# Ten instead of six channel blocks of two MLP jobs get their bias on VectorE, under a new written-out order

## The chip, the cores and the metric

One core of a Trainium2 chip. The metric is the device time of one execution in microseconds (us), the median of several runs. The engines are named as in the profile: PE (TensorE matmul) with PEld (its weight loads), DVE (VectorE), ACT (ScalarE), POOL (GpSimd) and SP (SyncE, which issues nearly all DMAs).

## The reference

Two layer kinds run in turn, twice: sliding-window attention (32 heads of 16 channels, a window of 256) and an MLP of 512 to 1792 channels with GELU, each on normalized rows, each added to the residual. There are 2048 rows of 512 channels in bfloat16, and both rounds use the same weights.

```python
def _A_ref(x, wqkv, wo):          # H = 32, Dh = 16, W = 256
    q, k, v = ...                 # x @ wqkv, split by heads
    scores = einsum("bhqd,bhkd->bhqk", q, k) * (Dh ** -0.5)
    mask = (idx[:, None] - idx[None, :] >= 0) & (idx[:, None] - idx[None, :] < W)
    p = softmax(where(mask, scores, -1e9))
    return einsum("bhqk,bhkd->bhqd", p, v) ... @ wo

def _B_ref(x, w1, b1, w2, b2):
    return gelu(x @ w1 + b1) @ w2 + b2

x = x + _A_ref(_layernorm(x), A_wqkv, A_wo)
x = x + _B_ref(_layernorm(x), B_w1, B_b1, B_w2, B_b2)
x = x + _A_ref(_layernorm(x), A_wqkv, A_wo)
x = x + _B_ref(_layernorm(x), B_w1, B_b1, B_w2, B_b2)
```

## The kernel before

**Tiles.** The rows stay on the chip in `X` as 16 tiles of 128 rows; two rounds make 32 tile steps (`tau` 0 to 31). Attention goes by 16 blocks `b` of two tiles. The MLP goes by ten jobs (`JOBS`): jobs 0 and 1 have two tiles each (256 columns), jobs 2 to 7 four (512 columns), jobs 8 and 9 two again.

**Attention of a block.** PE makes scores into pairs of PSUM banks (`sa`, `sb`); ACT takes exp from there into the ring `E` (L948), 304 times over the whole kernel. DVE or POOL multiplies the window's triangular parts by a mask (L969). PE multiplies by V (`od`), DVE transposes the result from PSUM (`TT`, L1034), takes reciprocals (`Rc`), DVE or POOL scales (`TM`, L1039), DVE transposes back (`OT`, L1044), and PE does the out-projection (`op`) that DVE adds to `X` (L790).

**LayerNorm rows** (`layernorm`, L734 to L760). DVE takes the statistics, POOL the power -1/2 (L741), DVE scales into `xn` (L744). For the first tiles PE then transposes the rows with the identity (L36). From `tau` 14 on in the attention layer, and for `tau` 4 to 29 in the MLP layer, VectorE transposes 32x32 blocks into one of four slots `xs_` (L753); SP writes the slot to a scratch tensor in DRAM, `scr_x` (L758), and reads it back in the wanted arrangement into `xnTA` (attention) or `xnTB` (MLP) (L760). Each is one DMA of 128 KB. SP issues in order and waits at the head of its queue: a read behind another waits with it.

**An MLP job** (`mlp`). For each of 14 channel blocks of 128, PE multiplies W1 by the job's rows. The first `NPRE` blocks go through VectorE: it adds the bias while it moves the block from PSUM to `gT` (L1103), and ACT takes GELU of two such blocks at a time from SBUF (L1106). The remaining blocks go to ACT straight from PSUM, bias and GELU in one (L1114). `NPRE` is 6 for all jobs but the last two, which have none. ACT loads a table at each turn from exp to GELU and back. Then PE multiplies by W2 (`y`) and DVE adds to `X`.

**The order** is written out by hand, as three lists that a planner made outside the kernel. `ORDER` names every piece of work once, and each engine executes its pieces in that order. `TURNS` says for each piece that two engines can do (masks, `TM`, some PSUM moves, the copy `xv`, the epsilon) which one does it: 0 is the first choice, DVE throughout, 1 the other. `BANKS` gives each PSUM group its banks. The durations that the code gives to each piece (`dur`) estimate when it starts and ends; in the finished program they only affect which PE instruction carries a wait that comes early, and the order of waits.

Of the kernel before, what the change touches and what calls it, by code (L numbers as in the profile page):

```python
# [298 lines left out]
def bass_interleave_layers__sliding_block__dense_activation_gelu__prompt_kernel(  # L299
# [43 lines left out]
    NXV = 1  # L343
# [16 lines left out]
    def NPRE(J):  # L360
        return 6
# [13 lines left out]
    with ExitStack() as kctx:  # L375
        S_ = _Sched(nc, kctx)

        def sb(name, shape, dtype=dt.bfloat16):
# [18 lines left out]
        xv = sb("xv", [P, NXV, DC, P])  # L397
        b1raw = xv[0:FC, 0, 0, :]
        scr = nc.dram_tensor("scr_x", (NSC, P, D), dt.bfloat16, kind="Internal").ap()
# [233 lines left out]
        add = PL.add  # L633
# [5 lines left out]
            reads=["ident"], writes=["ident"])  # L639
# [518 lines left out]
        B = PL.gmap  # L1158
# [52 lines left out]
```

## Time and profile before

| What | us |
|---|---|
| Median of three runs | 450.91 (450.76 to 451.44) |
| The profiled execution | 454.36 |
| Its span, first to last instruction | 452.6 |
| PE busy | 436.2 |
| ACT busy | 391.5 |
| DVE busy | 365.2 |
| POOL busy | 244.9 |

The rows of the trace come from the profiled execution, which is 3.45 us longer than the median. Busy time of PE is counted from a matmul's start to its modelled end, and neighbours overlap; so a matmul of 512 columns is listed with 380 ns while the next starts 216 ns after it. In a row of the groups the two numbers behind the bar are busy time in us and the mean length of one instruction in ns; behind the next bar stands the idle time of the engine just before them and what ended it. In the windows each engine's busy time stands with its count of instructions; `PEclk` is the granted share of TensorE's full clock.

### The profile page before, as it was taken

The numbers are of one execution on the slowest core, as the hardware profiler recorded it, in microseconds if no ns is written. First come the engines' busy times: TensorE is split into PE (matmuls) and PEld (weight loads), VectorE is DVE, ScalarE is ACT, GpSimd is POOL, SyncE is SP. The second block draws the span as 40 slices with busy tenths as digits, with TensorE's granted clock in tenths as the row PEclk, the third lists the DMA queues.
The fourth block names the chain that finished last, engine by engine and source line by source line (L and its number), as shares of the span: only waits on it lengthen the run. The fifth ranks groups of instructions, "written<-read, shape, count | busy, mean of one in ns | idle before, by whom it ended". The sixth has DMA issues, their size and how long they took to land.

```text
span 452.6 us, 19312 instructions
## 1 busy us (share of the span) xinstructions
PE 436.2 (96%) x8764; PEld 230.9 (51%) x8764; DVE 365.2 (81%) x733; ACT 391.5 (87%) x470; POOL 244.9 (54%) x297
## 2 busy tenths in 40 slices
PE   8999999888989999999999999999999999999997
PEld 5555645545534544554445535445454553445665
DVE  6999979789978889879987989998787787673711
ACT  3999999999969999799998999979998999793352
POOL 5674763626755555553587446662767365665120
PEclk9999999999989999999999999999999999999999
DMA  8920000000130112110040011400121002002102
GB/s 262 369 82 4 4 3 3 4 3 26 38 84 1 38 50 72 38 49 3 25 108 15 13 48 40 96 15 23 50 73 50 3 25 73 26 4 83 48 1 71
DMA packets 39903, 22.88 MB, mean 51 GB/s; under 512 B 24460, under 2 KB 39308, under 8 KB 39820
## 3 DMA queue, kind: packets, MB, share of 16 engines
q1 hardware_dynamic: 39404, 21.24, 16.2%
q8 instruction: 69, 1.13, 1.1%
q10 hardware_dynamic: 416, 0.39, 0.2%
q14 instruction: 14, 0.11, 0.1%
HBM read 13.77 MB, written 7.86 MB: 48 GB/s over the span
## 4 chain that ended last, share of the span: by engine, by line
PE 74%; ACT 13%; DMA 5%; DVE 4%; SPq 1%; issue 1%; POOL 0%; DVEq 0%
PE ps L32 74%; ACT E L948 11%; DMA xnTB<-scr_x 2%; DMA X<-in_A_x_dram 2%; DMA scr_x<-xs_ 1%; DVE stat L734 1%; DVE E L969 1%; SPq L760 1%; ACT gT L1114 1%; DVE xs_ L753 1%; SPq L698 1%; DVE KT L864 1%; PE ps L36 1%; DVE xn L744 0%; ACT gT L1106 0%
## 5 line engine op out<-in xcount | busy, mean ns | idle before, releaser
L948 ACT ACTIVATE E<-ps 128x1024 bf16<-128x1024 f32 x304 | 285.9, 1047 | 23.2 <-PE ps L32 22.4
L969 POOL TENSOR_TENSOR E<-E,mask 128x512 bf16<-128x512 bf16 (+1 forms) x138 | 145.6, 1069 | 89.4 <-DVE E L969 26.8
L32 PE MATMUL ps<-xnTB,W_sb 128*128 128x512 bf16 (+1 forms) x560 | 116.0, 340 | 3.4 <-DMA xnTB<-scr_x 3.1
L32 PE MATMUL ps<-W_sb,gT 128*128 128x512 bf16 (+1 forms) x462 | 118.1, 374 | 0.0
L32 PEld LDWEIGHTS ps<-xnTB,W_sb 128*128 128x128 bf16 x560 | 51.6, 98 | 48.2 <-ACT E L948 4.2
L32 PE MATMUL ps<-xnTA,Wqkv_sb 128*128 128x256 bf16 (+1 forms) x544 | 73.6, 267 | 1.5 <-ACT E L948 0.8
L32 PE MATMUL ps<-QT,KT 32*64 32x320 bf16 (+4 forms) x2976 | 65.5, 259 | 3.1 <-ACT E L948 1.7
L790 DVE TENSOR_TENSOR X<-X,ps 128x512 bf16<-128x512 bf16 x63 | 42.7, 679 | 29.5 <-PE ps L32 29.1
L1114 ACT ACTIVATE gT<-ps,b1T 128x512 bf16<-128x512 f32 (+1 forms) x92 | 47.8, 590 | 20.9 <-PE ps L32 20.7
L32 PEld LDWEIGHTS ps<-W_sb,gT 128*128 128x128 bf16 x462 | 40.4, 98 | 42.7 <-issue 6.9
L32 PEld LDWEIGHTS ps<-xnTA,Wqkv_sb 128*128 128x128 bf16 x544 | 47.3, 98 | 23.8 <-ACT E L948 3.4
L1034 DVE STREAM_TRANSPOSE TT<-ps 128x1024 f32<-128x1024 f32 x32 | 39.9, 1248 | 17.9 <-PE ps L32 17.4
L32 PEld LDWEIGHTS ps<-QT,KT 32*64 32x64 bf16 x2976 | 27.5, 103 | 50.0 <-ACT E L948 33.0
L1078 POOL TENSOR_TENSOR X<-X,b2b 128x512 bf16<-128x512 bf16 x32 | 36.7, 1155 | 29.4 <-DVE E L969 14.7
L969 DVE TENSOR_TENSOR E<-E,mask 128x512 bf16<-128x512 bf16 (+1 forms) x124 | 47.8, 415 | 2.2 <-ACT E L948 2.1
L32 PE MATMUL ps<-E,Va 64*17 64x128 bf16 (+3 forms) x3872 | 46.0, 229 | 2.8 <-issue 0.8
L32 PEld LDWEIGHTS ps<-E,Va 64*17 64x17 bf16 x3872 | 36.8, 85 | 20.5 <-PE ps L32 8.2
L741 POOL TENSOR_TENSOR statmv<-statmv,mhalf 128x1 f32<-128x1 f32 x64 | 36.6, 574 | 18.7 <-DVE statmv L738 15.6
L734 DVE BATCH_NORM_STATS2 stat<-X 128x6 f32<-128x512 bf16 x64 | 42.7, 677 | 3.1 <-DMA X<-in_A_x_dram 2.7
L864 DVE TENSOR_TENSOR KT<-ps,parmask 128x1024 bf16<-128x1024 f32 x30 | 36.1, 1208 | 4.7 <-PE ps L32 4.4
L1103 DVE TENSOR_SCALAR gT<-ps,b1T 128x512 bf16<-128x512 f32 (+1 forms) x48 | 31.4, 668 | 10.2 <-PE ps L32 9.9
L32 PE MATMUL ps<-Wo_sb,OT 128*128 128x512 bf16 x128 | 37.2, 380 | 0.4 <-ACT E L948 0.4
(56 smaller groups left out, 334.3 us busy)
## 6 DMA issues: line engine op xcount, KB each, us to landing
scr_x<-xs_ SPq DMA_DIRECT2D x44, 128.0 KB, 1.8
W_sb<-in_B_w_dram SPq DMA_DIRECT2D x2, 1792.0 KB, 15.8
xnTB<-scr_x SPq DMA_DIRECT2D x26, 128.0 KB, 2.9
xnTA<-scr_x SPq DMA_DIRECT2D x18, 128.0 KB, 2.4
out_dram<-X SPq DMA_DIRECT2D x15, 128.0 KB, 1.8
Wqkv_sb<-in_A_wqkv_dram SPq DMA_DIRECT2D x4, 256.0 KB, 5.2
X<-in_A_x_dram SPq DMA_DIRECT2D x1, 1024.0 KB, 8.9
Wqkv_sb<-in_A_wqkv_dram SPq DMA_DIRECT2D x1, 512.0 KB, 6.7
```

What stands on the lines that cost most here:

```text
L32: return self.e.matmul(*a, **k)
L36: return self.e.transpose(*a, **k)
L734: add("dve", lambda e, B: e.bn_stats(stat6[:, k6, :], X[:, t, :]), 590, reads=["X%d" % t], writes=["st%d" % k6], prio=prio)
L741: add("pool", lambda e, B: e.tensor_tensor(out=statmv[:, k, 1:2], in0=statmv[:, k, 1:2], in1=mhalf[:], op=ALU.pow), 535, reads=["ve%d" % k ...
L790: add("dve", lambda e, B: e.tensor_tensor(out=X[:, t, :], in0=X[:, t, :], in1=ps[:, B[g][0], :], op=ALU.add), d_psum(512), reads=["X%d" % ...
L864: add("dve", lambda e, B, g=g, i=i: e.tensor_tensor(out=KT[:, kb, :, 2 * i : 2 * i + 2, :].rearrange("p a c q -> p a (c q)"), in0=ps[:, B[ ...
L948: add("act", lambda e, B, g_=g_, gi=gi: e.activation(E[:, 2 * gi : 2 * gi + 2, e0 : e0 + 512], ps[:, B[g_][0] : B[g_][0] + 2, :], AF.Exp, ...
L969: op = lambda e, B, Ew=Ew, Mw=Mw: e.tensor_tensor(out=Ew, in0=Ew, in1=Mw, op=ALU.mult)
L1034: add("dve", lambda e, B: e.transpose(TT[:, s].rearrange("p a c q d -> p a (c q d)"), ps[:, B[g][0] : B[g][0] + 2, :].rearrange("p a n -> ...
L1078: add("pool", lambda e, B: e.tensor_tensor(out=X[:, t, :], in0=X[:, t, :], in1=b2b[:], op=ALU.add), 1110, reads=["X%d" % t, "b2b"], writes ...
L1103: add("dve", lambda e, B, g=g, fc=fc: e.tensor_scalar(out=gT[:, fc, 0:M], in0=ps[:, B[g][0], 0:M], scalar1=b1T[:, fc : fc + 1], scalar2=No ...
L1114: add("act", lambda e, B, g=g, fc=fc: e.activation(gT[:, fc, 0:M], ps[:, B[g][0], 0:M], AF.Gelu_apprx_tanh, bias=b1T[:, fc : fc + 1], scal ...
```

## The change

It is announced as: "LayerNorm rows moved chip to chip, four transfers a tile, no scratch in DRAM; ten channel blocks of two MLP jobs by VectorE ahead of GELU; new order". The diff has the second and the third part. The code that moves LayerNorm rows is the same but for a planner's duration: the rows still go through the scratch in DRAM, one write and one read a tile.

- `NPRE` is 10 for jobs 0 and 1, so VectorE adds the bias of four more blocks in each, and ACT takes them in pairs.
- The three lists are new. `ORDER` has 3263 entries instead of 3275: the twelve fewer are those of `NPRE` (a block that goes through VectorE is cut into two pieces on PE instead of four). The counts of all other pieces stay. `TURNS` moves some to other engines: POOL does 142 masks (138 before), 24 `TM` (18) and 32 epsilons (27); ACT does 13 moves of Q (11), 2 of the early `xnTA` (3) and 5 copies `xv` (7); DVE does the others.
- Two durations that only the planner reads are changed.

```diff
     def NPRE(J):
-        return 6
+        return 10 if J < 2 else 6
...
         ORDER = [
-            18, 21, 22, 23, 24, 25, 26, 27, 28, 29, 8, 0, 9, 10, 15, 19, 35, 20, 16, 17, 3, 4, 5, 1, 2, 6, 14, 36,
...
                 dma(lambda e, B: e.dma_start(scr[v], xs_[:, z, :]),
                     ["scr%d_0" % v], reads=["xs%d" % z], prio=prio, dur=2200.0 + room, issue=400.0)
                 dma(lambda e, B: e.dma_start(dst.rearrange("p r d j -> p r (d j)"), flat.rearrange("(r p c) -> p r c", r=4, p=P)),
-                    [dname], reads=["scr%d_0" % v], prio=prio, dur=2700.0 + room, issue=400.0)
+                    [dname], reads=["scr%d_0" % v], prio=prio, dur=2700.0 + 2 * room, issue=400.0)
...
                     pair_ = (xv[:, tau % NXV].rearrange("p d (r j) -> p r d j", r=4), rows(b, j))
-                    add("dve", lambda e, B, pair_=pair_: e.tensor_copy(*pair_), 300, reads=[xr[j]], writes=["xv%d" % (tau % NXV)],
+                    add("dve", lambda e, B, pair_=pair_: e.tensor_copy(*pair_), 190, reads=[xr[j]], writes=["xv%d" % (tau % NXV)],
```

Around the rows of job 2 (tiles 4 to 7) the lists differ as follows. Before, SP issues: tile 7's write, tile 5's read, tile 6's write, then the reads of tiles 6, 4 and 7; VectorE transposes tile 7, then tile 6, then adds the residual of tile 3. After, SP issues: tile 5's write and read, tile 4's write and read, the writes of tiles 6 and 7, a write of tile 14, then the reads of tiles 7 and 6; VectorE transposes tile 6, adds the residual of tile 3, then transposes tile 7.

421 rows, old and new, of tables (BANKS, ORDER, TURNS) are left out of this document.

## The prediction

> **What bounds the kernel now.** I read the page's head first, then cut the span into five stretches at places that the timeline shows: the first exp on ScalarE (12.39), the end of the first ScalarE-bound part (124.46), the end of the stretch with the low clock (135.78), the last matmul (449.83).
>
> ```profile
> span 452.6 us, 19312 instructions
> PE 436.2 (96%) x8764; PEld 230.9 (51%) x8764; DVE 365.2 (81%) x733; ACT 391.5 (87%) x470; POOL 244.9 (54%) x297
> ```
> ```profile
> core 0: us, PE busy (x) PEld busy (x) DVE busy (x) ACT busy (x) POOL busy (x), PEclk, DMA share, GB/s
> 0.00:12.39 12.39, 10.69 (x104) 6.60 (x105) 8.05 (x22) 4.71 (x8) 5.72 (x22) 1.00 0.91 269
> 12.39:124.46 112.07, 104.10 (x2515) 59.98 (x2513) 101.94 (x214) 109.72 (x130) 67.47 (x83) 1.00 0.16 51
> 124.46:135.78 11.32, 9.20 (x224) 3.71 (x224) 8.08 (x15) 7.69 (x9) 5.81 (x7) 0.85 0.34 84
> 135.78:449.83 314.05, 312.20 (x5924) 160.58 (x5924) 246.71 (x484) 269.41 (x325) 165.91 (x186) 1.00 0.15 41
> ```
>
> The share of the whole span (PE 96%) hides that two engines take turns. From 12.39 to 124.46 ScalarE is busy 109.72 of 112.07 us: it is the bound, PE has 8.0 us of idle time, VectorE 10.1, GpSimd 44.6. From 135.78 PE is busy 312.20 of 314.05, and ScalarE has 44.6 us free: there only matmuls, changes of tile shape and late operands count. Between the two lie 11 us in which something else is last. The chain that ended last and PE's timeline say what:
>
> ```profile
> 119.51 0.72 DVE xs_ L753
> 120.25 3.87 DMA scr_x<-xs_
> 124.14 0.37 SPq L760
> 124.55 0.51 SPq L760
> 125.11 2.97 DMA xnTB<-scr_x
> ```
> ```profile
> 125.88 0.43 PE L32 MATMUL ps<-QT,KT 32*64 32x64 bf16 x24
> 128.12 2.54 PE L32 MATMUL ps<-xnTB,W_sb 128*128 128x512 bf16 x6 [1.81 <-DMA xnTB<-scr_x]
> 130.59 0.65 PE L32 MATMUL ps<-QT,KT 32*64 32x256 bf16 x16
> ```
>
> PE has nothing to do for 1.81 us before the first group of MLP job 2 (tiles 4 to 7), which waits for its normalized rows: transposed by VectorE, written to DRAM (3.87 us to landing), then read back, with three reads queued one behind the other on SP. Behind this wait the granted clock averages 0.85 over 11.32 us: 0.15 x 11.32 = 1.7 us of full-speed matmul time lost. That is why six matmuls take 2.54 us there.
>
> **The change part by part.** It edits one number (NPRE), planner durations, and the three lists. The planner durations reach the program only through which PE instruction carries a wait, so I cost them at nothing; if the waits moved badly, the price is in term f. I matched the entries of both lists to the code, entry by entry, and count from that.
>
> (a) *GELU of jobs 0 and 1.* Four more channel blocks of each job (8 in all, 256 columns wide) get their bias on VectorE; ScalarE then takes them in pairs.
>
> ```profile
> L1114 ACT ACTIVATE gT<-ps,b1T 128x256 bf16<-128x256 f32 x44 | 18.1, 479 | 19.6 <-PE ps L32 19.4
> L1106 ACT ACTIVATE gT<-gT 128x512 bf16<-128x512 bf16 x6 | 3.8, 651 | 0.0
> L1103 DVE TENSOR_SCALAR gT<-ps,b1T 128x256 bf16<-128x256 f32 x12 | 5.4, 472 | 0.6 <-PE ps L32 0.6
> L969 DVE TENSOR_TENSOR E<-E,mask 128x512 bf16<-128x512 bf16 x105 | 42.9, 440 | 2.2 <-ACT E L948 2.1
> L969 POOL TENSOR_TENSOR E<-E,mask 128x512 bf16<-128x512 bf16 x113 | 129.3, 1158 | 76.2 <-DVE E L969 24.1 <-DVE xn L744 20.7 <-ACT E L948 14.9
> L1039 DVE TENSOR_TENSOR TM<-TT,Rc 128x512 bf16<-128x512 f32 x14 | 9.6, 687 | 0.1
> L1039 POOL TENSOR_TENSOR TM<-TT,Rc 128x512 bf16<-128x512 f32 x18 | 19.0, 1058 | 19.6 <-DVE Rc L1037 9.1 <-DVE E L969 5.7 <-DVE xn L744 4.3
> ```
>
> Instructions in a row overlap a little, so I divide busy time by count. Eight direct GELUs go: 8 x 18.1/44 = 3.29 us. Four paired ones come: 4 x 3.8/6 = 2.53. ScalarE does 0.76 us less, all inside the stretch that it bounds, and its table switches stay at 17 in the list. A chain leads from exp through masks, PV and out-projection to the rows of job 2, so this reaches the end of the stretch: **-0.8 us**. Bounds: 0 (if VectorE is last there) and, with all of ScalarE's idle time of that stretch (112.07 - 109.72 = 2.35), -3.1.
>
> (b) *VectorE and GpSimd.* The eight bias additions cost VectorE 8 x 5.4/12 = 3.6 us before job 2. In the same part of the list it gives 4 wide masks (4 x 0.44 = 1.8) and 2 TM products (2 x 0.69 = 1.4) to GpSimd, so it stays about level: 0, hidden by its 10.1 idle us. GpSimd gets those at its own price: 4 x 1.16 + 2 x 1.06 = 6.8 us, against 44.6 idle. Over the whole list it has 6 TM products and 4 masks more. I take **0**, since the cover is six times the load; the other end is that some stand on the chain, a mask or TM late by one long operation (1.16) each. That is the rival below.
>
> (c) *Order of the rows of job 2.* SP and VectorE in the trace of before:
>
> ```profile
> 119.21 0.32 SPq L758 DMA_DIRECT2D scr_x<-xs_  x1
> 119.57 0.43 SPq L760 DMA_DIRECT2D xnTB<-scr_x  x1
> 120.25 0.36 SPq L758 DMA_DIRECT2D scr_x<-xs_  x1
> 124.14 1.47 SPq L760 DMA_DIRECT2D xnTB<-scr_x  x3
> ```
> ```profile
> 118.48 0.70 DVE L753 STREAM_TRANSPOSE xs_<-xn 128x512 bf16<-128x512 bf16 x1
> 119.51 0.71 DVE L753 STREAM_TRANSPOSE xs_<-xn 128x512 bf16<-128x512 bf16 x1
> 120.15 0.65 DVE L790 TENSOR_TENSOR X<-X,ps 128x512 bf16<-128x512 bf16 x1
> ```
> ```profile
> DMA to landing us min/median/max: 1.7/2.3/4.3
> ```
>
> (The last row groups the moves to and from the scratch.) The slow write, 3.87 us, was issued right behind a read of 128 KB, and tile 7's read stood in SP's queue behind the read that waited for that write. In the new list the reads of tiles 4 and 5 are issued well before the writes of tiles 6 and 7, so both writes should land in near the 2.3 us of the median, and tile 7's read goes ahead of tile 6's. Against it: tile 7's transpose now stands on VectorE behind the residual of tile 3, which waits for that tile's last matmul (0.65 plus the wait), and a write for tile 14 stands between on SP, whose transpose needs an SBUF slot that tile 6's write must have left. My count on the old clock: residual at 118.5, transpose done 119.9, write landed 122.3, read issued 122.8, landed near 125.8, tile 6's near 126.3; PE is free for job 2 at 126.3 - 0.4 (its work ahead of that group is 0.38 us shorter) = 125.9. Leaves about 0.4 of 1.81: **-1.4**. Bounds: -1.8, and +0.4 if the write takes 3.9 to 4.3 again.
>
> (d) *The clock.* If PE no longer stands still for about two microseconds there, I expect the 1.7 us back: **-1.7**; bounds 0 and -1.7. [...]
>
> (e) *Matmuls and later waits.* Matmuls are the same in number and size. Consecutive groups start at:
>
> ```profile
> 133.95 1.04 PE L32 MATMUL ps<-Wqkv_sb,xnTA 128*128 128x512 bf16 x4
> 134.82 0.59 PE L32 MATMUL ps<-xnTB,W_sb 128*128 128x512 bf16 x2
> 135.35 0.42 PE L32 MATMUL ps<-QT,KT 32*64 32x256 bf16 x16
> ```
> ```profile
> PE ps L32 <- DMA xnTB<-scr_x: 3.1, 3, 1.8
> ```
>
> Four matmuls take 0.87, so two 0.435; with a change of shape behind them they take 0.53: 0.095 a change. The list has 362 changes instead of 368, but only 2 of the 6 lie behind the start of job 2, where PE is the bound: **-0.2**. Of PE's three waits for rows, 1.3 us (3.1 - 1.8) belong to jobs 3 and 5. For job 3 the last transpose has three VectorE operations fewer ahead of it; for job 5 nothing clear changes: **-0.5**, bounds 0 and -1.3.
>
> (f) *Everything else that a new order may miss.* PE's idle time in the ScalarE-bound stretch (8.0 us) and the 1.85 us from 135.78 on are what an order of this kind leaves. I add **+1.0**, an eighth of the 8.0; bounds 0 and +3, nothing in the rows fixing it more closely.
>
> Sum: -0.8 + 0 - 1.4 - 1.7 - 0.2 - 0.5 + 1.0 = -3.6 us. The profiled execution took 454.36 us, span 452.6; the median of the runs is 450.91, 0.8% under the profiled one, and I carry the difference over unscaled: **447.3 us**.
>
> **The rivals.** *Clock by another cause.* The wait shrinks, the half clock comes anyway. Against it: no other stretch of the windows has a clock under 1.00, and this one begins with the wait. Time: 447.3 + 1.7 = 449.0.
>
> *The wait moves or stays.* The new place of tile 7's transpose costs what the better queue gains; (c), (d) and the -0.5 go. 450.91 - 0.8 - 0.2 + 1.0 = 450.9: no change. For it speaks how close the need is: two transfers of 2.3 with issue and queue take near 6 us, and the list gives tile 7 about that from its transpose on.
>
> *Slower: GpSimd is late.* Its place is before job 2, where ScalarE and PE feed on masks and out-projections: each long operation of GpSimd that stands ahead of one that a PV group or an out-projection needs makes it 1.16 late, and later rows make PE's wait at job 2 stay. One gives 452.1, two give 450.9 + 2.3 = 453.2; with the wait unchanged it decides from the first one. For it: GpSimd already stood idle for VectorE before masks (24.1 + 20.7 us in the row), so its operations run at VectorE's convenience. Against: 44.6 idle us. [...]
>
> *The change isn't what its words say.* They speak of rows moved on the chip by four transfers a tile. The diff keeps the scratch, and the new list has the same 44 writes and 44 reads. Were the words true after all, the 3.1 us of waits and the clock loss would go: 450.91 - 3.1 - 1.7 - 0.8 - 0.2 + 1.0 = 446.1.
>
> **How the numbers follow.** Forecast 0.47; clock by another cause 0.08; wait stays 0.13 (0.12 of it within 0.2%, 0.01 slower); GpSimd late 0.29; words true 0.03. 0.2% is 0.9 us, about what a measurement of this kernel can tell from no change. Faster: 0.47 + 0.08 + 0.03 = 0.58; same 0.12; slower 0.30. The range goes up to the slower rival with two operations, 453.2, and down to where (c) and (a) come near their ends: -0.8 - 1.2 (half of ScalarE's idle time) - 1.8 - 1.7 - 0.2 - 0.5 = -6.2, 444.7. Cases of both signs hold much of the chance; the forecast's own range is 444.7 to 449.9.
>
> **What would show it.** Right: PE's wait for the rows of job 2 under 1 us; no stretch with a granted clock under 1.00; job 2's first matmul at 125 to 126 us instead of 128.12; 84 direct and 28 paired GELUs; PE busy again over 99% from there. Wrong: a PE wait of over 1.5 us for a mask, an out-projection or rows; a longer TT-to-OT path; a first exp later than 12.4, which shifts all of the ScalarE-bound stretch and which I cost at nothing, as the work ahead of it is the same; or PE idle of over 3 us behind 136 us.

## The result, and the profile after

| | Kernel before | Kernel after |
|---|---|---|
| Median of 19 runs, us | 451.44 (450.76 to 454.13) | 449.34 (448.11 to 450.80) |
| Ratio, 95% interval | | 0.9952 (0.994 to 0.9964) |
| The profiled execution, us | 454.36 | 449.27 |

The kernel after is faster by 2.1 us, 0.48%. A second comparison, on another occasion, gave 0.9954 (0.9937 to 0.9971). The forecast was 447.3 in a range of 444.7 to 453.2: the sign and the range held, and the time came out 2.0 us above the forecast. The profiled execution of before lay 2.9 us above the median of these 19 runs, while that of after lies on its own, so the two profiles differ by 5.1 us where the kernels differ by 2.1.

The head of the page of after, and its windows at the same times (busy time and count of PE, PEld, DVE, ACT, POOL, then the granted clock):

```profile
span 447.2 us, 19238 instructions
PE 424.6 (95%) x8691; PEld 232.0 (52%) x8764; DVE 366.2 (82%) x727; ACT 389.5 (87%) x465; POOL 253.5 (57%) x312
```
```profile
12.39:124.46 112.07, 102.38 (x2516) 60.61 (x2532) 105.01 (x219) 110.43 (x129) 75.29 (x93) 1.00 0.17 54
124.46:135.78 11.32, 10.57 (x282) 5.37 (x281) 9.47 (x18) 10.63 (x12) 7.94 (x8) 1.00 0.21 49
135.78:444.40 308.62, 300.78 (x5809) 159.45 (x5864) 243.60 (x471) 264.38 (x319) 164.84 (x190) 1.00 0.15 41
```

In the first row ScalarE is still the bound (110.43 of 112.07), VectorE is busy for 105.01 us (before 101.94), and GpSimd for 7.8 us more. A part of this is only that after gets further in the program by 124.46 us: counted from the first scores to job 2, VectorE is busy for 106.10 us in before and 106.47 in after. In the second row the clock is 1.00 instead of 0.85 and PE is busy 1.4 us longer in the same 11.32 us. In the third PE seems less busy than before; but 73 of its 8764 matmuls have no record in this trace, which leaves false gaps (5.2 us of PE's idle time in this stretch has no releaser; with these counted as busy it is at 99.1%, as forecast). Step by step, after is 0.53 us later than before at the first scores, has gained 2.7 us from there to job 2 and 3.3 from there to the last matmul, 1.7 of them the half clock.

Groups of the same instructions as in the prediction, different shapes apart:

```profile
L1114 ACT ACTIVATE gT<-ps,b1T 128x256 bf16<-128x256 f32 x36 | 15.4, 474 | 17.2 <-PE ps L32 17.2
L1106 ACT ACTIVATE gT<-gT 128x512 bf16<-128x512 bf16 x10 | 6.0, 624 | 0.0
L1103 DVE TENSOR_SCALAR gT<-ps,b1T 128x256 bf16<-128x256 f32 x20 | 8.9, 471 | 0.3
L969 POOL TENSOR_TENSOR E<-E,mask 128x512 bf16<-128x512 bf16 x112 | 127.6, 1156 | 69.0 <-DVE xn L744 20.9 <-DVE E L969 20.4 <-ACT E L948 17.5
L1039 POOL TENSOR_TENSOR TM<-TT,Rc 128x512 bf16<-128x512 f32 x24 | 25.4, 1058 | 34.1 <-DVE Rc L1037 13.0 <-DVE xv L876 7.4 <-DVE xn L744 6.1
```

Eight direct GELUs fewer (44 to 36), four paired ones more (6 to 10), eight bias additions more (12 to 20): as counted. Together with the wider ones there are 84 direct and 28 paired.

The chain of waits to the rows of job 2 in the kernel after, and PE's timeline there:

```profile
119.54 3.19 DMA scr_x<-xs_
122.75 0.37 SPq L760
123.16 2.75 DMA xnTB<-scr_x
125.95 3.13 PE ps L32 x88
```
```profile
125.95 1.47 PE L32 MATMUL ps<-xnTB,W_sb 128*128 128x512 bf16 x6 [0.45 <-DMA xnTB<-scr_x]
```

The chain is the same one, 2.17 us earlier at its end. A write still takes 3.19 us, but now only one read stands between it and the rows, and PE waits 0.45 instead of 1.81 us. The six matmuls take 1.47 instead of 2.54 us, since no half clock follows.

### The profile page after: what moved, and what is told of

It reads as the page before. It is cut to its first block, busy times and chain, and to the rows that moved or that the text cites. A ratio compares the mean times of both kernels' runs of the same rounds, so it can differ in the third digit from the quotient of the medians.

```text
span 447.2 us, 19238 instructions
## 1 busy us (share of the span) xinstructions
PE 424.6 (95%) x8691; PEld 232.0 (52%) x8764; DVE 366.2 (82%) x727; ACT 389.5 (87%) x465; POOL 253.5 (57%) x312
## 4 chain that ended last, share of the span: by engine, by line
PE 68%; ACT 25%; DVE 3%; issue 2%; DMA 1%; SPq 0%
PE ps L32 67%; ACT E L948 18%; ACT gT L1114 2%; ACT gT L1106 2%; ACT L948 1%; ACT L1106 1%; DMA scr_x<-xs_ 1%; DMA xnTB<-scr_x 1%; ACT L1114 1%; DVE KT L864 0%; PE ps L36 0%; DVE X L790 0%; DVE xs_ L753 0%; DVE E L969 0%; DVE Va L720 0%
## 5 line engine op out<-in xcount | busy, mean ns | idle before, releaser
L969 POOL TENSOR_TENSOR E<-E,mask 128x512 bf16<-128x512 bf16 (+1 forms) x142 | 147.2, 1055 | 86.8 <-DVE E L969 26.9
L32 PE MATMUL ps<-W_sb,gT 128*128 128x512 bf16 (+1 forms) x421 | 110.4, 373 | 4.8 <-issue 3.6
L1114 ACT ACTIVATE gT<-ps,b1T 128x512 bf16<-128x512 f32 (+1 forms) x84 | 45.1, 602 | 23.5 <-PE ps L32 23.4
L1039 POOL TENSOR_TENSOR TM<-TT,Rc 128x512 bf16<-128x512 f32 x24 | 25.4, 1058 | 34.1 <-DVE Rc L1037 13.0
L1103 DVE TENSOR_SCALAR gT<-ps,b1T 128x512 bf16<-128x512 f32 (+1 forms) x56 | 35.4, 645 | 7.1 <-PE ps L32 6.7
```

Source lines behind the costliest of these rows:

```text
L32: return self.e.matmul(*a, **k)
L969: op = lambda e, B, Ew=Ew, Mw=Mw: e.tensor_tensor(out=Ew, in0=Ew, in1=Mw, op=ALU.mult)
L1039: mul = lambda e, B: e.tensor_tensor(out=TM[:, sm].rearrange("p c q a d -> p a (c q) d"), in0=TT[:, s, :, :, :, 0:Dh].rearrange("p a c q d ...
L1103: add("dve", lambda e, B, g=g, fc=fc: e.tensor_scalar(out=gT[:, fc, 0:M], in0=ps[:, B[g][0], 0:M], scalar1=b1T[:, fc : fc + 1], scalar2=No ...
L1114: add("act", lambda e, B, g=g, fc=fc: e.activation(gT[:, fc, 0:M], ps[:, B[g][0], 0:M], AF.Gelu_apprx_tanh, bias=b1T[:, fc : fc + 1], scal ...
```

## The experiments

Line numbers in some of these kernels are one smaller than in the kernels before and after. All ratios are to the kernel before, run beside them. In the short diffs of SP's queue W is a write to the scratch, R a read, and the number is the tile.

**Two identical programs.** The kernel before again, under a name of its own.

```diff
+# same program
```

> The kernel before, unchanged. Theory (the half clock behind job 2's wait came in the profiled execution and not in most others): ratio 1.000 within 0.2%, a granted clock of 0.999 or 1.000 and a span near 449.5 us in most executions, 0.996 with 452 to 453 us in a few; PE's wait for the rows of job 2 is there in the new profile (1 to 2 us). Rival (the half clock belongs to this order): 0.996 in most executions, and spans near 452.6 beside times near 451.4.

Ratio 1.0014 (0.9991 to 1.0037), no half clock ahead of the last matmul in its profile although PE waited 1.62 us for the rows of job 2:

```profile
128.31 1.47 PE L32 MATMUL ps<-xnTB,W_sb 128*128 128x512 bf16 x6 [1.62 <-DMA xnTB<-scr_x]
```

So the wait belongs to that kernel, and the half clock to some of its executions. The ratio also says how well medians of 12 runs compare: the copy came out 0.9 us above the kernel that it copies.

How often the half clock comes can be counted, since every run lists its mean granted clock, and the 3.41 us at a clock of 0.50 in the profile of before (128.36 to 131.77 us) are 0.5 x 3.41 / 450 = 0.0038 of it. Of 111 runs of the kernel before with such a record, 12 show 0.996, the rest 0.999 or 1.000. Ten of the 12 are among the 47 runs on one chip, two among the 64 on two others. On the first, in the 35 runs beside these experiments, the median of the six at 0.996 was 453.7 us, and of the 24 at 1.000 it was 451.7. So it costs 2.0 us where it comes, and moves the median little (452.0 with the six, 451.7 without). None of 25 runs of the kernel after shows 0.996 or less; but six of these were on a chip where before shows it in one run of 29, so these counts alone do not show that after is free of it.

**NPRE alone.** The order of before, eight more bias additions on VectorE right behind their matmuls, and a paired GELU at the place of the later of two direct ones.

```diff
-        return 6
+        return 10 if J < 2 else 6
```

> The order, engines and banks of before, with 10 blocks ahead of GELU in jobs 0 and 1: the new bias additions stand right behind their matmuls, each pair's GELU at the place of its later block. Theory (ScalarE bounds the stretch to 124 us): 0.5 to 0.8 us faster than before, ratio 0.998 to 0.999, and job 2's rows that much earlier. Rival (VectorE is just as full there): no change, 0.999 to 1.001, or slower by up to 2 us, since the old order left no place for eight more additions on VectorE.

Slower: 1.0033 (1.0012 to 1.0054), and 1.0 us above the identical copy (453.94 and 452.95). ScalarE's timeline in this run, in its first run of GELUs, and VectorE's just before:

```profile
54.55 1.28 ACT L1113 ACT_TABLE_LOAD   x1
55.84 0.47 ACT L1113 ACTIVATE gT<-ps,b1T 128x256 bf16<-128x256 f32 x1
57.68 0.63 ACT L1105 ACTIVATE gT<-gT 128x512 bf16<-128x512 bf16 x1 [1.36 <-DVE gT L1102]
```
```profile
54.79 1.28 DVE L733 BATCH_NORM_STATS2 stat<-X 128x6 f32<-128x512 bf16 x2
55.98 0.30 DVE L735 BATCH_NORM_AGGREGATE statmv<-stat 128x2 f32<-128x6 f32 x2
56.39 1.65 DVE L1102 TENSOR_SCALAR gT<-ps,b1T 128x256 bf16<-128x256 f32 x4
```

VectorE works on the statistics of the next tiles while ScalarE stands idle for 1.36 us, with its GELU table loaded, until the bias additions are done. That is more than the 0.8 us that the pairs save. The scores of block 3 start 2.5 us later than in the second run of before (93.03 and 90.50 us); 0.45 of that was there at the first scores of block 0.

**The queue alone.** The kernel before, with SP's order around job 2 changed and nothing else.

```diff
-  SP: W5 W4 W7 R5 W6 R6 R4 R7
+  SP: W5 W4 R5 R4 W7 W6 R7 R6
```

> The kernel before; on SP alone the reads of tiles 4 and 5 go ahead of the writes of tiles 6 and 7, and tile 7's read ahead of tile 6's... both behind those writes. Theory (a write behind a read lands late, and reads queue behind it): the write of tile 6 lands in 2 to 2.5 us instead of 3.87, PE's wait for the rows of job 2 falls from 1.81 to under 0.5 us, no half clock, the median 1.0 to 1.8 us faster than before (ratio 0.996 to 0.998). Rival (VectorE's transposes set the wait, not the queue): wait 1.5 us or more, ratio 0.999 to 1.001.

Faster: 0.9962 (0.9942 to 0.9982). SP's queue and PE at the last reads:

```profile
120.91 3.06 SPq L760 DMA_DIRECT2D xnTB<-scr_x  x2
```
```profile
126.20 1.47 PE L32 MATMUL ps<-xnTB,W_sb 128*128 128x512 bf16 x6
```

PE no longer waits there, nor (beyond 0.3 us) at any later job. The way was not quite as expected: the write of tile 6 still took 3.36 us to land, with no read issued right ahead of it. What went is the queue behind it: the last read was issued at 123.60 instead of 125.11 and, with the one ahead of it nearly landed, took 2.24 instead of 2.97 us. The wait of job 3 (0.76 us in the second run of before) fell too, so job 3 started 57.6 us after job 2 instead of 58.4.

**The kernel after with the old kind of queue.**

```diff
-  SP: W5 R5 W4 R4 W6 W7 W14 R7 R6
+  SP: W5 W4 W6 R5 W7 W14 R7 R4 R6
```

> The kernel after; on SP alone tile 5's read goes back behind tile 6's write (ahead of tile 7's) and tile 4's read behind tile 7's read. Theory: tile 7's write lands in 3.5 to 4 us, PE's wait for the rows of job 2 is 1.5 to 2.5 us, the median 1.0 to 2.0 us above the kernel after (ratio to before 0.997 to 1.000), more where the clock halves. Rival: the wait stays at about 0.5 us and the ratio at 0.995.

0.9944 (0.9925 to 0.9964), against 0.9952 and 0.9954 for after: not slower. PE's wait in this run, and in a second run of the kernel after:

```profile
127.53 1.47 PE L32 MATMUL ps<-xnTB,W_sb 128*128 128x512 bf16 x6 [0.97 <-DMA xnTB<-scr_x]
```
```profile
126.45 1.47 PE L32 MATMUL ps<-xnTB,W_sb 128*128 128x512 bf16 x6 [1.07 <-DMA xnTB<-scr_x]
```

So in the order of after the place of the two early reads is worth nothing that can be measured. The unchanged kernel after itself waited 0.45 us in one execution and 1.07 in another, so a wait of 0.97 is within what it does by itself.

**The new order without NPRE.**

```diff
-        return 10 if J < 2 else 6
+        return 6
```

> The kernel after with 6 blocks ahead of GELU again: the four pieces of each direct block stand where its two stood, its GELU where its bias addition stood (in job 1 the blocks are renumbered so that all direct GELUs fall into ScalarE's GELU run); order, engines and banks else as after. Theory (ScalarE bounds that stretch, so 8 direct GELUs against 4 paired ones cost 0.8 us): ratio to before 0.996 to 0.998, the start of job 2 about 0.8 us later than after. Rival (the ten blocks are worth nothing, the gain is the queue's and the order's): within 0.1% of after, 0.994 to 0.996.

1.0010 (0.9994 to 1.0025): no gain is left, which neither expectation had. The second run of GELUs lasts from table load to table load, in the trace of this run:

```profile
85.79 1.28 ACT L1106 ACT_TABLE_LOAD   x1
90.38 1.20 ACT L1114 ACTIVATE gT<-ps,b1T 128x256 bf16<-128x256 f32 x3 [0.33 <-PE ps L32]
92.12 1.28 ACT L948 ACT_TABLE_LOAD   x1
```

That is 6.33 us, against 5.47 in the kernel after. Job 2 starts 2.3 us later than in the first run of after, of which 0.4 is there at the first scores, and 1.8 later than in the second; the two runs of GELUs account for 1.3 of it. A part of that may be this edit's own: the blocks were put into an order that had been laid out for ten.

**TM products back on their engines of before.** Of the 32, 14 change sides; GpSimd has 18 instead of 24.

```diff
-  TURNS of TM: 24 on GpSimd
+  TURNS of TM: 18 on GpSimd, as in the kernel before
```

> The kernel after, the TM products on the engines that before used (18 on GpSimd instead of 24; 14 of them change sides). Theory (GpSimd's idle time hides them): ratio 0.994 to 0.997, no step of the kernel moved by more than 0.3 us. Rival (a TM on GpSimd holds up out-projections): 0.990 to 0.993.

0.9993 (0.9976 to 1.0009), that is 1.8 us slower than after (0.0041 x 451). Work given to GpSimd is a part of the gain, not a cost. The loss is spread: this run's profile is 1.1 us behind that of after at job 2 and 2.8 behind at the last matmul (446.95 and 444.13).

**Tile 7's transpose ahead of the residual of tile 3**, in the kernel after.

```diff
-  DVE: X3 += op; ... transpose tile 7
+  DVE: transpose tile 7; X3 += op
```

> The kernel after; on VectorE tile 7's transpose goes ahead of the residual of tile 3. Theory (what is left of the wait hangs on tile 7's write, which starts behind that residual): PE's wait for the rows of job 2 falls from 0.45 us to under 0.2, ratio 0.993 to 0.996 (0.3 to 0.5 us under after). Rival (tile 6's read, behind tile 7's on SP, or its write's landing sets it): wait as after.

0.9967 (0.9951 to 0.9983), no gain. SP's queue and PE in this run:

```profile
118.34 3.98 SPq L758 DMA_DIRECT2D scr_x<-xs_  x3
123.19 0.92 SPq L760 DMA_DIRECT2D xnTB<-scr_x  x2
```
```profile
126.35 1.46 PE L32 MATMUL ps<-xnTB,W_sb 128*128 128x512 bf16 x6 [0.64 <-DMA xnTB<-scr_x]
```

The write of tile 7 was issued at 119.39, took 3.79 us, and the read behind it was issued at 123.19, where after has 122.75. So in this trace the residual ahead of tile 7 is not what keeps PE waiting: the landing of the write, not the transpose, ends last.

**Two PSUM moves from ScalarE to VectorE**, on top of the last edit (`Q1_2` at 94 us, `xb1_1` at 74 us).

```diff
-  TURNS of Q1_2, xb1_1: ScalarE
+  TURNS of Q1_2, xb1_1: VectorE
```

> As e7_tile7_first, and two PSUM moves of the ScalarE-bound stretch (one of Q at 94 us, one of xnTB at 74 us) from ScalarE to VectorE. Theory (ScalarE is the bound there and VectorE has 7 us free): 0.5 to 1.1 us under e7_tile7_first, ratio 0.991 to 0.994. Rival (VectorE's order is as full as ScalarE's there): same as e7_tile7_first or up to 1 us above.

1.0004 (0.9981 to 1.0026): what ScalarE is spared, the chain through VectorE loses. PE waited 1.04 us for the move, and the granted clock was 0.50 from 97.31 us on. PE's timeline and two windows of this run, then the same two windows around the half clock in the profile of before (in the windows: length, PE busy, and towards the end the granted clock):

```profile
94.82 0.74 PE L32 MATMUL ps<-E,Va 64*17 64x64 bf16 x64 [0.65 <-DVE E L969]
96.60 0.42 PE L32 MATMUL ps<-QT,KT 32*64 32x256 bf16 x16 [1.04 <-DVE QT L720]
```
```profile
93.90:97.31 3.41, 1.72 (x123) 1.12 (x128) 2.86 (x8) 2.11 (x4) 1.43 (x2) 1.00 0.02 5
97.31:104.14 6.83, 5.71 (x94) 2.79 (x80) 3.99 (x9) 5.42 (x6) 2.51 (x5) 0.50 0.01 2
```
```profile
124.95:128.36 3.41, 1.60 (x30) 0.58 (x31) 3.41 (x8) 3.41 (x4) 2.44 (x3) 1.00 0.73 192
128.36:131.77 3.41, 3.41 (x24) 0.90 (x22) 0.82 (x2) 0.62 (x2) 2.88 (x4) 0.50 0.37 81
```

The clock is 0.50 for 6.83 us here and for 3.41 us in before, and in the 3.41 us ahead of it PE was busy for 1.72 and 1.60 us. Of its twelve runs, five show a mean clock of 1.000 (median 451.5), three 0.996 (452.6) and four 0.992 (453.9): some 1.2 us for each 0.004 of mean clock.

**NPRE and the queue together, in the order of before.**

```diff
-        return 6
+        return 10 if J < 2 else 6
...
-  SP: W5 W4 W7 R5 W6 R6 R4 R7
+  SP: W5 W4 R5 R4 W7 W6 R7 R6
```

> The kernel before with both single edits: NPRE 10 for jobs 0 and 1 (as in the run of NPRE alone, ratio 1.0033) and SP's order for the rows of job 2 (as in the run of the queue alone, 0.9962). Theory A, the parts add up and VectorE's load is the price of NPRE in the old order: 0.9962 + 0.0033 = 0.9995, with job 2's first matmul at about 128.7 us (126.20 in the queue run plus the 2.5 us that NPRE alone cost at the start of block 3) and no PE wait over 0.5 us for its rows. Theory B, the queue's wait hid what NPRE saves on ScalarE, and shows it once gone: 0.9945 or less, job 2 at 125.5. Which one decides whether the new order around jobs 0 and 1 is needed for the gain.

1.0017 (1.0004 to 1.003): additive (0.9995) or a little worse, and far from 0.9945. ScalarE's wait of 1.4 us for the bias is there again, PE has no wait at job 2, and one is back at job 3:

```profile
185.95 1.90 PE L32 MATMUL ps<-xnTB,W_sb 128*128 128x512 bf16 x8 [1.23 <-DMA xnTB<-scr_x]
```

The two parts of the change that can be named don't make the gain together in the order of before. But one of them nearly does so alone: 0.9962 (0.9942 to 0.9982) for the queue can't be told from 0.9952 for the whole change. In the order of before the ten blocks lose what the queue gains; to have them without that loss takes another order.

**NPRE 12 in the order of after.**

```diff
-        return 10 if J < 2 else 6
+        return 12 if J < 2 else 6
```

> The kernel after with NPRE 12 instead of 10 for jobs 0 and 1: four more bias additions on VectorE, placed right behind their matmuls, and two more paired GELUs in place of four direct ones. Theory A, ScalarE alone bounds the stretch to 124 us: -0.4 us against the kernel after (4 x 0.41 gone, 2 x 0.63 come), about 0.994. Theory B, VectorE is level with ScalarE there (17.02 of 17.60, 14.74 of 15.00 and 14.50 of 15.00 us busy from 12.4 to 60 us): four additions of 0.45 us cost up to 1.8 us, so 0.996 to 0.999, with the scores of block 3 up to 1.8 us later than in the kernel after run beside it.

0.9987 (0.9973 to 1.0001), 2.0 us slower than the kernel after on the same chip (451.32 and 449.32). ScalarE's second run of GELUs:

```profile
85.09 1.28 ACT L1105 ACT_TABLE_LOAD   x1
87.41 1.67 ACT L1105 ACTIVATE gT<-gT 128x512 bf16<-128x512 bf16 x3 [0.39 <-DVE gT L1102]
89.79 0.63 ACT L1105 ACTIVATE gT<-gT 128x512 bf16<-128x512 bf16 x1 [0.36 <-DVE gT L1102]
91.32 1.28 ACT L947 ACT_TABLE_LOAD   x1
```

Six pairs in place of five, and yet 6.23 us instead of 5.47: ScalarE stands idle for VectorE's bias additions, as in the run of NPRE alone.

**NPRE 12, and four masks from VectorE to GpSimd.**

```diff
-  TURNS of four wide masks between jobs 0 and 1: VectorE
+  TURNS of four wide masks between jobs 0 and 1: GpSimd
```

> As the run with NPRE 12, and four wide masks between jobs 0 and 1 moved from VectorE to GpSimd (4 x 0.44 = 1.8 us off VectorE, 4 x 1.16 = 4.6 us on GpSimd, which is 8.22 of 15.00 us busy from 30 to 45 us). If VectorE is the limit and GpSimd the room, this gives back what NPRE 12 cost: within 0.5 us of the kernel after run beside it, or up to 0.4 better. If GpSimd's long masks come late for PV, it is 1 us or more slower than the run with NPRE 12 alone.

1.0009 (0.9996 to 1.0022), 0.7 us slower still, though the intervals overlap. PE waited for one of the masks. The first four lines are masks of GpSimd and VectorE ahead of that wait:

```profile
67.33 1.15 POOL L968 TENSOR_TENSOR E<-E,mask 128x512 bf16<-128x512 bf16 x1 [0.22 <-ACT E L947]
67.97 0.80 DVE L968 TENSOR_TENSOR E<-E,mask 128x512 bf16<-128x512 bf16 x1
72.16 0.40 DVE L968 TENSOR_TENSOR E<-E,mask 128x512 bf16<-128x512 bf16 x1
72.23 1.33 POOL L968 TENSOR_TENSOR E<-E,mask 128x512 bf16<-128x512 bf16 x1 [0.53 <-DVE xn L743]
73.66 1.62 PE L32 MATMUL ps<-E,Va 64*17 64x64 bf16 x128 [0.98 <-POOL E L968]
```

This is the shape of the slower rival of the prediction, one late operation of GpSimd on the chain, made by giving GpSimd masks without regard to when PE needs them. Single masks also took longer than others of their size here: VectorE's at 67.97, begun while GpSimd was in one, 0.80 us where the one at 72.16 took 0.40, and GpSimd's at 72.23, the one that PE waited for, begun while VectorE was in one, 1.33 where the one at 67.33 took 1.15. So this run does not show whether NPRE 12 lacked time on VectorE or only had its additions in the wrong place.

**The kernel after again.**

> The kernel after again, on the chip of the two runs with NPRE 12, to compare with them directly: 0.994 to 0.9965. Its profile gives the positions of the steps once more; executions of one kernel have differed by about 1 us at the start of block 3.

0.9954 (0.9937 to 0.9971). The first scores of block 0 started at 12.65 us (12.43 in the first profile), those of block 3 at 89.18 (89.30), job 2 at 126.45 (125.95), the last matmul at 444.61 (444.13).

No kernel among these is measurably faster than after.

## Why the prediction came out as it did

**(a) GELU, -0.8: right, and on conditions that it didn't state.** In the traces a run of GELUs goes from one table load to the next. The first of the two, in the second run of before, then in after:

```profile
54.09 1.28 ACT L1114 ACT_TABLE_LOAD   x1
59.98 1.28 ACT L948 ACT_TABLE_LOAD   x1
```
```profile
54.22 1.28 ACT L1106 ACT_TABLE_LOAD   x1
59.69 1.28 ACT L948 ACT_TABLE_LOAD   x1
```

5.89 us became 5.47, and the second run (85.46 to 91.35, then 84.70 to 90.17) the same: -0.84 for both, where -0.76 was worked out. But the saving is had only where the bias additions are done before ScalarE comes to them. With the pieces in their old places VectorE cost 1.36 us at one wait. The prediction looked for VectorE's price in its sum of busy time; it lies in where the additions stand in VectorE's queue.

**(b) VectorE and GpSimd, 0: right as a term; idle time was no reason for it.** From the first scores to job 2 VectorE is busy for 106.10 us in before and 106.47 in after (105.82 and 107.08 in the second pair), so it stayed about level, as forecast. But that its idle time hides eight additions does not follow from a sum: in the run of NPRE alone it had idle time too, and they cost 1.36 us at one wait. GpSimd late, the rival with a chance of 0.29, did not happen: no wait of PE in the trace of after names GpSimd, and with the products back on their engines of before the kernel was 1.8 us slower.

In the mean GpSimd's wide masks took the same, 1156 ns each in after and 1158 in before. Single masks of VectorE varied: thirteen in the trace of after began more than 0.05 us ahead of the end of a mask of GpSimd, all of them ended 0.15 to 0.35 us behind it, and seven took 0.60 to 1.13 us, where the mean of the wide ones is 0.44. In before seven took 0.55 to 0.99 us. All of these long ones stand behind 126 us, where PE is the bound, so nothing shows that the change paid for them. The idle time before GpSimd's masks, which the prediction counted for this rival, is another thing: in after the profile puts at least 41.3 us of 69.0 down to operations of VectorE that released them (20.9 and 20.4 in the row above), and in before 44.8 of 76.2.

**(c) The rows of job 2, -1.4: the wait shrank, by less in the mean, and by another way.** The wait went from 1.81 to 0.45 us (0.4 was forecast) and job 2 began at 125.95 (125 to 126). In the second pair of profiles it went from 1.62 to 1.07, so -1.4 is the better of two pairs, and their mean is -0.95. The prediction blamed the slow write on the read right ahead of it and expected 2.3 us; without such a read it took 3.19 and 3.88 us in the two traces of after. The queue behind it was what counted in the order of before, where the queue edit alone took the wait away; in the order of after, the same reads put late cost nothing. That the wait can stay near 1 us without a loss in the median remains unexplained; the medians don't resolve less than about 0.2%.

**(d) The clock, -1.7: this is the step that failed.** The half clock went, but it had not been in the ordinary execution. It came in 12 of 111 runs of before. The profiled execution of before had it, and the prediction both subtracted its 1.7 us and carried the profiled execution's excess over the median (3.45 us) over in full, so the same microseconds were taken off twice. Without (d) the sum is -1.9 us, and -2.1 was measured. That these are so close is partly luck, since (c), (e) and (f) were off by several tenths each and in both directions.

A wait of 1.81 us (before), and waits of 0.65 and 1.04 us close together (the run with two moves less on ScalarE), were followed by half clock; one of 1.62 us (the second run of before) was not. The rival "clock by another cause" had no stretch to its name in after, ahead of the last matmul.

**(e) Later waits and shapes, -0.7: too small.** From the first matmul of job 2 to the last of all it took 319.66 us in the second run of before, 318.18 and 318.16 in the two of after: -1.5. Of that, 0.76 is the wait at job 3 and 0.47 the one at job 5, for which the prediction saw no change:

```profile
186.69 1.90 PE L32 MATMUL ps<-xnTB,W_sb 128*128 128x512 bf16 x8 [0.76 <-DMA xnTB<-scr_x]
```

Both went in after, and in the queue run too, where only SP's order around job 2 was changed. So the term was the right one, but the waits went whole (1.2 us, close to the bound of -1.3) and not by 0.5; with the -0.2 of the shapes, 1.4 of the 1.5 is accounted for.

**(f) Unforeseen, +1.0: a part of it was there.** The first exp came at 12.92 us instead of 12.39, which the prediction listed as a sign of being wrong and had costed at nothing. The first scores started 0.53 us later too. Executions of one order differ by as much, but the order seems to have a share: in the five traces with the order of before the first scores came at 11.70 to 12.54 us (mean 12.0), in the nine with that of after at 11.90 to 12.80 (mean 12.5). No run tests it. Between first scores and job 2 the profile of after is 2.7 us shorter than that of before (113.5 against 116.2); (a) and (c) make 2.2 of it.

The steps of the profiles don't add up to the medians. The second run of before against the mean of the two of after gives +0.5 us to the first scores, -2.6 from there to job 2 and -1.5 from there on, together -3.6, where the medians differ by 2.1. Both profiled executions of before were longer than its medians (454.36 and 452.81 against 451.4 to 452.0), and where an ordinary one is shorter is not shown.

**The other rivals.** "The wait stays" did not happen in after; the old kind of queue and the second execution of after, with waits of about 1 us, suggest that more of it could have stayed without harm. That the words of the change are true was excluded by the trace: its rows go through the scratch as before.

What stays open is why the new order without NPRE, and TM on its old engines, each lose nearly all of the gain, when the first names 0.8 us of work on ScalarE. The new banks, and the masks and small operations that changed engines, were not tried by themselves. Each of these edits takes something out of an order that was made with it in place, so their losses don't add up to the gain, and none of them is the worth of that part by itself.

## What to carry to other kernels

A saving on the bound engine is worth its arithmetic only if the work that replaces it stands early enough in the other engine's queue: look for the first instruction of the bound engine that would wait, not at the other engine's share of busy time. Where one profiled execution lies above the median of the runs, find out what in it is not ordinary (a stretch at half clock here) before a term of the sum is built on it. In a queue that issues in order, a transfer that is ready should not stand behind one that waits for a landing: in the order of before that alone was worth about 1.7 us of 452, most of the gain of the whole change, in the order of after nothing that could be measured.

## What the runs showed of the hardware that was not expected

In the trace of before the granted clock was 0.50 for 3.41 us from 128.36 us on, and in the run with two moves less on ScalarE for 6.83 us from 97.31 us on. In the 3.41 us ahead of these PE was busy for 1.60 and 1.72 us, with no single wait over 1.81 us. In the second run of before PE was busy for 1.80 of 3.42 us around its wait for the rows of job 2, and the clock behind it was 1.00, with six matmuls in 1.47 us:

```profile
125.36:128.78 3.42, 1.80 (x31) 0.66 (x32) 3.42 (x8) 3.42 (x4) 2.40 (x3) 1.00 0.73 192
```

What decides whether the clock falls is not shown by these three cases.

In the trace of after the longest mask of VectorE that began while GpSimd was in a mask took 1.13 us, where the mean of VectorE's wide masks is 0.44. In the run with four masks moved, a mask of GpSimd that began while VectorE was in one took 1.33 us, where another of its size took 1.15. What makes some of them long was not tested.

In the trace of after, 28 writes of 128 KB to the scratch were issued with no other transfer of SP outstanding: 19 of them landed in 1.68 to 1.76 us, the other nine in 2.13 to 3.36. The second of the two writes ahead of job 2 is a slow one in all fourteen traces (2.59 to 3.97 us, with 3.19 in the first of after and 3.87 in that of before), and what makes it so was not found.
